# Value matmuls of sixteen attention units in four quarters of the array, with a new instruction order

## The chip, the cores and the metric

The kernel runs on one core of a Trainium2 chip. The metric is the device time of one execution in microseconds; lower is better. Engines are called by their rows in the profile: PE is TensorE (PEld its weight loads), DVE is VectorE, ACT is ScalarE, POOL is GpSimd, and SP is the queue that issues the transfers.

## What is computed

Attention over 4 batches of 8 heads, 768 positions and 64 elements a head, followed by a gated convolution. Each query sees its neighbours within 16 positions and one summary of each of the 24 blocks of 32 positions; the result, with the heads side by side (512 wide), goes through a gate and two 512x512 products.

```python
k_sum = k.reshape(B, H, nb, block, D).max(axis=3)
v_sum = v.reshape(B, H, nb, block, D).mean(axis=3)
scores_l = scale * np.matmul(q, k.transpose(0, 1, 3, 2))
mask_l = np.abs(pos[:, None] - pos[None, :]) < window
scores_s = scale * np.einsum('bhsd,bhnd->bhsn', q, k_sum) + np.log(block)
a = softmax(np.concatenate([np.where(mask_l, scores_l, -1e9), scores_s], axis=-1))
x = np.matmul(a, np.concatenate([v, v_sum], axis=2))
...
for k in range(K):
    gate_pre += conv_w[k][None, None, :] * xp[:, k:k + S, :]
gate = 1.0 / (1.0 + np.exp(-gate_pre))
val = x @ w_val
return gate * val @ w_out
```

## The kernel before, in words

The work is cut into 24 units, numbered 0 to 23 in the code: 4 batches x 3 thirds of a sequence (256 queries) x 2 halves of the heads (two head pairs, r = 0 and 1). Two units make a group g, 0 to 11, in which all 512 columns of 256 positions are there. The order of everything is written out by hand: the string `ORDER` is a list of words, each one call of a small function with its numbers, and each engine runs its share of the calls in that order. Waits between engines come from the data alone.

A unit u goes through these words. `s` (L519) multiplies queries by 120 keys, 16 matmuls in the four quarters of the array (two row halves for the heads, two column halves for the queries). `n` (L536) adds the mask on DVE, eight steps with the row maximum; `e` (L555) takes the exponentials on ACT; `r` (L562) the row sums and reciprocals on DVE; `m` (L567) scales on POOL. `t` (L576) transposes on PE into one PSUM bank, once for each r, and `c` (L581) copies it out on ACT. `x` (L588) multiplies by the values: 16 matmuls of 120 rows into 64 columns each, in the two column halves of the array, into one bank of its own:

```python
dst = xp(u)[h * D : (h + 1) * D, r, i * QT : (i + 1) * QT]
src = pts(u)[:, TPU * r + 2 * (i // 2) + h, (i % 2) * QT : (i % 2 + 1) * QT]
nc.tensor.matmul(dst, v[:KW, i, c0 : c0 + D], src, start=True, stop=g > 0)
```

PE takes an fp32 matmul in two passes, so the trace has 32 records for these 16 calls, and two for each other fp32 one that is no transpose. `Y` (L609) copies x to SBUF on ACT, `X` (L605) writes its rounded head there too, and `Z` (L613) the rest on POOL. `I` (L622) starts the gate with the newest tap on ACT, `T` (L629) adds four more taps on DVE, four dependent instructions for each r, and `G` (L638) takes the tanh on ACT.

A group then goes through `v` (L642, x times w_val, four calls of 12 matmuls), `gf` (L655, gate times val on DVE), `gh` and `gl` (L663, L666, its head on ACT and rest on POOL), `o` (L674, times w_out, two calls), `ob` and `O` (scale on ACT, store). Group 0 computes in plain fp32 with the joined weights `wf` (four calls of `val`, and eight of `out`, each of 128 columns); the other groups use the split weights. The weights come as 64-bit numbers that ACT and DVE turn to fp32: `rb` on ACT, `sh` (L363) and `or` (L367, the join) on DVE, four blocks for each matrix. `ks` (L221) takes the block maxima of the keys on DVE, `kc` (L233) writes them between the keys on POOL, `vp` (L271) sums the blocks of the first batch's values on DVE, `tv` (L244) those of the others on POOL.

Of the eight PSUM banks, scores have two, transposes one, x one, the gate one, and val, out and some small products share three.

Of the kernel before, what the change touches and what calls it, by code (L numbers as in the profile page):

```python
# [22 lines left out]
QT = 64  # L23
# [13 lines left out]
KALLOC = OFF_A + 2 * STEP * (NT // 2 + 1)  # L37
# [7 lines left out]
LATE_INIT = (2, 3, 4, 5)  # L45
# [4 lines left out]
DVE_COPY = ()  # L50
POOL_V = ()
POOL_LOW = ()
# [3 lines left out]
Lk0.0 wz Lk0.1 Mu ez cv W0 Lp0 W1 Lc W2 W3 W4 Lk0.2 W5 Lp1 W6 W7 W8 Mm Lp2 ks0.0 Lk0.3 ks0.1 Lp3  # L56
W9 W10 shc kc0.0 W11 W12 s0.0 W13 n0.0 kc0.1 W14 Ln1 s0.1 ks0.2 W15 e0.0 n0.1 Ln0 kc0.2 ks0.3
W16 s1.0 e0.1 kc0.3 Mi W17 n1.0 r0 vp1.1 W18 W19 s1.1 m0.0 e1.0 n1.1 Lq1 vp0.0 vp1.0 rbc e1.1
t0.0 s2.0 vc1.1 c0.0 s2.1 Lwv1 Ln3 m0.1 vp0.1 vc1.0 vc0.0 vc0.1 W20 W21 t0.1 vb0 hal0 W22 n2.0
shwv1 Lv0 n2.1 Ln2 rbwv1 orc c0.1 vbc0 orwv1 Lq2 Lwv2 W23 s3.0 s3.1 x0.0 e2.0 x0.1 r1 n3.0 vp3.0  # L60
n3.1 vp3.1 e2.1 wcwv1 I0 m1.0 m1.1 t1.0 Y0 vp2.0 vp2.1 r2 Lwv0 c1.0 e3.0 t1.1 Lwv3 Lv1 s4.0 T0.0
vc3.0 vc2.1 vc3.1 vc2.0 s4.1 vb1 n4.0 rbwv2 c1.1 vbc1 n4.1 x1.0 rbwv0 e3.1 rbwv3 wlwv1 m2.1 m2.0
shwv0 shwv2 s5.0 t2.0 x1.1 orwv0 shwv3 orwv2 orwv3 s5.1 Lk1.0 Lk1.1 n5.0 r3 c2.0 Y1 T0.1 n5.1
e4.0 wcwv3 e4.1 v0.1.0 t2.1 v0.0.0 G0 m3.1 wcwv2 Lk1.2 c2.1 wlwv3 m3.0 I1 r4 Lu1.2 v0.1.1 m4.0
F1 Lq3 t3.0 e5.0 m4.1 c3.0 v0.0.1 t3.1 x2.0 e5.1 ks1.1 x2.1 ks1.0 T1.0 c3.1 Lk1.3 wlwv2 X2 Y2
kc1.1 kc1.0 T1.1 ks1.2 t4.1 Lv2 Lu1.1 Lwo1 ks1.3 s6.0 Lq4 s6.1 hal1 tv1.2 x3.0 Lwo0 x3.1 G1 I2
c4.1 Z2 n6.1 n6.0 t4.0 gf0.1 r5 kc1.2 kc1.3 T2.0 X3 Y3 wcwv0 e6.0 s7.0 s7.1 n7.0 gf0.0 T2.1 Z3
# [46 lines left out]
def tile_attention_then_gated_conv(  # L114
# [69 lines left out]
    def ident_make():  # L184
# [619 lines left out]
```

## Time and profile before

| | us |
|---|---|
| median of 3 runs | 238.43 |
| the runs | 238.08 to 238.94 |
| profiled execution, span from its first to its last instruction | 236.1 |
| PE busy | 224.9 (95%) |
| ACT busy | 190.6 (81%) |
| DVE busy | 184.2 (78%) |
| POOL busy | 152.2 (64%) |

The profiled execution is one more execution than the three that were timed; the page gives its own time as the span, which holds nothing of what lies ahead of the first instruction and behind the last.
Busy time is that in which an engine works on an instruction. PE's matmuls are pipelined and overlap, so its busy time is a union of records. A view of waits tells for each engine which other engine's instruction ended its idle time; the chain of waits is followed back from the last instruction.

### The profile page before, as it was taken

To read this page: it belongs to the slowest core of one execution; us is meant where nothing else is said; L and a number is where in the kernel's file an instruction comes from. 1 tells how busy PE (TensorE), PEld (TensorE's weight loads), DVE (VectorE), ACT (ScalarE), POOL (GpSimd) and SP (SyncE) were. 2 spreads that over 40 slices of the span, in tenths; PEclk is the share of its full clock that TensorE was granted. 3 is DMA by queue.
4 is the path that set the end of the run, shared out by engine and by line. 5 is a ranking of instruction groups with operands and counts; after the bars stand their busy time and mean duration, and the time that the engine had idled before them with its cause. 6 is when DMAs were issued, how large, how long until landed. Compare 5 with 4: busy or idle time off the path is not lost.

```text
span 236.1 us, 7464 instructions
## 1 busy us (share of the span) xinstructions
PE 224.9 (95%) x2734; PEld 196.1 (83%) x2736; DVE 184.2 (78%) x698; ACT 190.6 (81%) x620; POOL 152.2 (64%) x222
## 2 busy tenths in 40 slices
PE   7777999998999999999999999999999999999994
PEld 2356787897999889998899799898889898898983
DVE  6899889999989999988899979839568765544710
ACT  2699899998899998999999989598979399347221
POOL 4246369998989896876658859963850845608030
PEclk9999999999999999999999999999999999999999
DMA  6999989939846789392757168711634420202212
GB/s 202 402 408 393 412 280 384 336 115 321 286 170 208 296 254 282 124 310 89 240 98 270 46 186 322 250 40 27 230 77 117 142 95 3 89 3 95 83 56 78
DMA packets 19812, 46.14 MB, mean 195 GB/s; under 512 B 2336, under 2 KB 7200, under 8 KB 19776
## 3 DMA queue, kind: packets, MB, share of 16 engines
q1 hardware_dynamic: 19776, 45.68, 56.6%
q8 instruction: 21, 0.34, 0.6%
q14 instruction: 15, 0.12, 0.1%
HBM read 37.21 MB, written 6.29 MB: 184 GB/s over the span
## 4 chain that ended last, share of the span: by engine, by line
PE 78%; DVE 14%; ACT 2%; DMA 2%; issue 1%; SPq 1%; POOL 0%; DVEq 0%; ACTq 0%; POOLq 0%
PE out L690 28%; PE val L653 24%; PE x L596 9%; PE pt L579 8%; PE s L528 8%; DVE g L633 4%; DVE sn L544 3%; DMA q<-in_qT_dram 2%; DVE ks L225 2%; DVE wf L367 2%; DVE wf L363 1%; PE x L598 1%; DVE gf L659 1%; ACT p L557 1%; SPq L204 1%
## 5 line engine op out<-in xcount | busy, mean ns | idle before, releaser
L633 DVE SCALAR_TENSOR_TENSOR g<-xf,cwt,g 128x256 f32<-128x256 f32 x192 | 93.7, 488 | 24.0 <-ACT g L627 12.7
L557 ACT ACTIVATE p<-sn,nm 128x120 f32<-128x120 f32 x192 | 73.3, 388 | 5.8 <-DVE nm L544 5.8
L569 POOL TENSOR_TENSOR p<-p,ri 128x480 f32<-128x480 f32 x48 | 47.3, 998 | 31.2 <-DVE ri L565 19.9
L653 PE MATMUL val<-xh,wv 128*128 128x256 f32 x352 | 50.8, 287 | 0.0
L653 PEld LDWEIGHTS val<-xh,wv 128*128 128x128 f32 x352 | 44.1, 189 | 0.3 <-issue 0.2
L690 PE MATMUL out<-wo,gh 128*128 128x512 f32 (+1 forms) x184 | 44.0, 381 | 0.0
L544 DVE CUSTOM_DVE_ANT_0 sn<-s,mask 128x120 f32<-128x120 f32 x192 | 41.5, 277 | 3.0 <-PE s L528 2.7
L667 POOL TENSOR_TENSOR gl<-gf,gh 128x512 fp32r<-128x512 f32 x22 | 28.1, 1287 | 21.8 <-ACT gh L664 21.7
L690 PEld LDWEIGHTS out<-wo,gh 128*128 128x128 f32 x184 | 32.8, 188 | 5.9
L586 ACT COPY pts<-pt 120x512 f32<-120x512 f32 x48 | 28.0, 584 | 11.6 <-PE pt L579 11.5
L557 ACT ACTIVATION_READ_ACCUMULATOR p<-sn,nm 128x1 f32 x192 | 37.1, 193 | 0.0
L579 PE MATMUL pt<-ident,p 128*120 128x128 f32 x192 | 30.0, 279 | 2.9 <-ACT pts L586 2.1
L615 POOL TENSOR_TENSOR xl<-xf,xh 128x512 fp32r<-128x512 f32 x22 | 28.4, 1296 | 3.9 <-ACT xf L611 3.2
L596 PE MATMUL x<-pts,v 120*64 120x64 f32 x768 | 30.2, 225 | 0.0
L596 PEld LDWEIGHTS x<-pts,v 120*64 120x64 f32 x768 | 26.2, 137 | 3.9 <-issue 1.5
L528 PE MATMUL s<-k,q 64*64 64x120 f32 x768 | 25.9, 269 | 2.1 <-POOL k L239 0.6
L579 PEld LDWEIGHTS pt<-ident,p 128*120 128x120 f32 x192 | 21.2, 137 | 7.8 <-POOL vpad L287 1.7
L253 POOL TENSOR_TENSOR vT<-vT 128x384 f32<-128x384 f32 (+3 forms) x44 | 25.9, 589 | 2.6
L653 PE MATMUL val<-xl,wv 128*128 128x256 f32 x176 | 27.5, 278 | 0.0
L528 PEld LDWEIGHTS s<-k,q 64*64 64x64 f32 x768 | 19.9, 132 | 7.2 <-issue 2.4
L659 DVE SCALAR_TENSOR_TENSOR gf<-gt,val 128x512 f32<-128x512 f32 x24 | 16.3, 679 | 10.5 <-PE val L653 10.1
L690 PE MATMUL out<-wo,gl 128*128 128x512 f32 (+1 forms) x92 | 23.8, 380 | 0.0
(64 smaller groups left out, 282.9 us busy)
## 6 DMA issues: line engine op xcount, KB each, us to landing
v<-in_vw_dram SPq DMA_DIRECT2D x24, 512.0 KB
k<-in_kT_dram SPq DMA_DIRECT2D x16, 478.0 KB
vT<-in_vT_dram SPq DMA_DIRECT2D x16, 384.0 KB
out_dram<-ob SPq DMA_DIRECT2D x23, 256.0 KB
q<-in_qT_dram SPq DMA_DIRECT2D x11, 512.0 KB
raw_wv<-in_wv_dram SPq DMA_DIRECT2D x4, 512.0 KB
raw_wo<-in_wo_dram SPq DMA_DIRECT2D x4, 512.0 KB
v<-vs SPq DMA_DIRECT2D x36, 48.0 KB
```

The lines of the kernel that those rows point to most:

```text
L528: nc.tensor.matmul(sp(u)[64 * e : 64 * e + 64, h, c * KW : c * KW + KW], qt(g)[64 * h : 64 * h + 64, pr, i * QT : i * QT + QT], ktile[b, p ...
L544: nc.vector.tensor_tensor_reduce(sn(u)[:, n, :], sp(u)[:, h, c * KW : c * KW + KW], mask[:, mv, :], -1.0 / math.sqrt(D), 3.0e38, ALU.add, ...
L557: nc.scalar.activation(pr_(u)[:, n, :], sn(u)[:, n, :], AF.Exp, bias=nm(u)[:, n : n + 1], scale=-1.0, accum_out=rs(u)[:, n, 0:1],)
L569: nc.gpsimd.tensor_tensor(pr_(u)[:, w], pr_(u)[:, w], st["ri", u][:, w].unsqueeze(2).broadcast_to([P, TPU, KW]), ALU.mult,)
L579: nc.tensor.transpose(pt[:KW, i, :], pr_(u)[:, TPU * r + i, :], ident)
L586: nc.scalar.copy(dst, src)
L596: nc.tensor.matmul(dst, v[:KW, i, c0 : c0 + D], src, start=True, stop=g > 0)
L615: nc.gpsimd.tensor_tensor(xl(g)[:, two(hp), :], xf(g)[:, two(hp), HALO:], xh(g)[:, two(hp), :].bitcast(F32), ALU.subtract,)
L633: nc.vector.scalar_tensor_tensor(gp(u)[:, r], xf(g)[:, pr, o : o + SG], cwt[:, pr, o : o + 1], gp(u)[:, r], ALU.mult, ALU.add,)
L653: nc.tensor.matmul(pp[:, r], w, x, start=(n == 0), stop=(n == len(terms) - 1))
L667: nc.gpsimd.tensor_tensor(gl(g)[:, two(cp), :], grp["gf", g, cp], gh(g)[:, two(cp), :].bitcast(F32), ALU.subtract)
L690: nc.tensor.matmul(pp, x, w, start=(n == 0), stop=(n == len(terms) - 1))
```

## The change

- `x` of units 4 to 19 (the fifth to the twentieth) is cut in two along its 120 rows: 64 and 56. Each of its matmuls becomes two, in two row halves of the array, so that the four quarters are used; the row halves write to two PSUM banks (`xp(u, 0)` and `xp(u, 1)`). `Y` copies the first to SBUF, and a new word `Ya` adds the second to it on DVE. `X` and `I` of these units read SBUF.
- The bank of x is given up: transposes and x take turns in two banks (`ps_t`, 2 buffers).
- Queries of group 0 stand behind the keys of batch 0 in one array (`kq`), so that four loads bring both. The weights are loaded by rows rather than by columns.
- `v` of group 0 is cut by the two units, `o` of group 0 by rows (one matmul of 512 columns for each call, added up over four calls).
- `n`, `e`, `T`, `I` and `r` are cut to smaller words, so that others can stand between their pieces. Some work changes its engine: 12 `X`, 12 `gh` and four weight casts go from ACT to POOL (`Xp`, `ghp`, `wcp`); 14 half `I`, five `Y`, two `X`, four `c` and five `ob` from ACT to DVE (`Id`, `Yd`, `Xd`, `cd`, `obd`); half of the value sums of batch 0 from DVE to POOL (`vt`). The scaled bits of w_val lie in PSUM.
- `ORDER` is another one.

The core of the diff (of `ORDER` and of what only renames or splits a function, a line or two):

```diff
-LATE_INIT = (2, 3, 4, 5)
+QUARTERS = tuple(range(4, 20))
+LATE_INIT = (2, 3, 4, 5) + QUARTERS
...
-W16 s1.0 e0.1 kc0.3 Mi W17 n1.0 r0 vp1.1 W18 W19 s1.1 m0.0 e1.0 n1.1 Lq1 vp0.0 vp1.0 rbc e1.1
+kc0.1 s0.1 W11 n0.1.1 n0.1.0 ks0.2 n0.0.0 n0.0.1 Lk0.3 Ln1 Lq1 Ln0 Ln3 Lc Lwv2 Ln2 Lwv0 ks0.3
...
-    ps_t = ctx.enter_context(tc.tile_pool(name="ps_t", bufs=1, space=bass.MemoryType.PSUM))
-    ps_x = ctx.enter_context(tc.tile_pool(name="ps_x", bufs=1, space=bass.MemoryType.PSUM))
+    ps_t = ctx.enter_context(tc.tile_pool(name="ps_t", bufs=2, space=bass.MemoryType.PSUM))
...
+        if b == 0:
+            nc.sync.dma_start(t, kq[pr])
+        else:
+            nc.sync.dma_start(t[:, :KTOT], kT[b - 1, pr])
...
+        if nm[:2] == "wv":
+            home, tag, bufs = ps_p, "pp", 3
...
-        nc.sync.dma_start(
-            raw.rearrange("p (k c) -> p k c", c=n), wcols[nm][:, :, k * n : k * n + n]
-        )
+        nc.sync.dma_start(raw, wrows[nm][k])
...
-    def xp(u):
-        return bank(ps_x, "x", u, [P, 2, SG])
+    def xp(u, half=0):
+        key = "x", u, half
+        if key not in st:
+            st[key] = ps_t.tile([P, 2, SG], F32, tag="pt", name=f"x_{u}_{half}")
+        return st[key]
...
+    def mm_x_quarters(u, r):
+        b, th, hp, g = of(u)
+        for i in range(TPU):
+            for half, rows in enumerate((slice(0, 64), slice(64, KW))):
+                for h in range(2):
+                    c0 = (2 * hp + r) * P + h * D
+                    nc.tensor.matmul(
+                        xp(u, half)[h * D : (h + 1) * D, r, i * QT : (i + 1) * QT],
+                        vtile[g][rows, i, c0 : c0 + D],
+                        pts(u)[rows, TPU * r + 2 * (i // 2) + h, (i % 2) * QT : (i % 2 + 1) * QT],
+                        start=True,
+                        stop=True,
+                    )
...
+    def x_head(u, eng=None):
+        b, th, hp, g = of(u)
+        src = xf(g)[:, two(hp), HALO:] if u in QUARTERS else xp(u)
+        (eng or nc.scalar.copy)(xh(g)[:, two(hp), :], src)
...
+    def x_add(u):
+        b, th, hp, g = of(u)
+        dst = xf(g)[:, two(hp), HALO:]
+        nc.vector.tensor_tensor(dst, dst, xp(u, 1), ALU.add)
...
+    def tap(u, r, o):
+        b, th, hp, g = of(u)
+        pr = 2 * hp + r
+        nc.vector.scalar_tensor_tensor(
+            gp(u)[:, r], xf(g)[:, pr, o : o + SG], cwt[:, pr, o : o + 1], gp(u)[:, r],
+            ALU.mult, ALU.add,
+        )
...
-            terms = [(grp["gf", g, ci // 2][:, ci % 2, rows], wblock(cb)[:, ci]) for ci in range(4)]
+            terms = [(grp["gf", g, cb // 2][:, cb % 2, rows], wf[:, cb])]
+            start, stop = cb == 0, cb == 3
...
-        "x": mm_x, "X": x_head, "Y": x_full, "Z": x_rest, "I": ginit, "T": taps, "G": gate,
+        "x": mm_x, "Ya": x_add, "X": x_head, "Y": x_full, "Z": x_rest, "I": ginit, "T": tap, "G": gate,
...
+        "cd": on(pcopy, dcopy), "Xd": on(x_head, dcopy), "Xp": on(x_head, pcast), "Yd": on(x_full, dcopy),
+        "ghp": on(g_head, pcast), "Id": on(ginit, scaled_dve), "obd": on(out_scale, scaled_dve),
```

What the new order does to two engines, at the places of which the prediction speaks. A name's number is that of a buffer's use; `x8` counts calls.

DVE ahead of the fourth join of the output weights (`wf<-sc_wo`, `wf`), before:

```order
L363 TENSOR_SCALAR wf<-raw_wo_771 128x512
L367 SCALAR_TENSOR_TENSOR wf<-sc_wo_952,wf 128x512
L363 TENSOR_SCALAR wf<-raw_wo_732 128x512
L367 SCALAR_TENSOR_TENSOR wf<-sc_wo_878,wf 128x512
L363 TENSOR_SCALAR wf<-raw_wo_924 128x512
L367 SCALAR_TENSOR_TENSOR wf<-sc_wo_981,wf 128x512
L659 SCALAR_TENSOR_TENSOR gf_0_1004<-gt_977,val_0_904 128x512
L564 TENSOR_REDUCE ri_1006<-rs_114 128x8
L565 RECIPROCAL ri_1006<-ri_1006 128x8
L249 TENSOR_REDUCE vsT_3_1027<-vT_3_1016 128x24
L363 TENSOR_SCALAR wf<-raw_wo_998 128x512
L367 SCALAR_TENSOR_TENSOR wf<-sc_wo_1009,wf 128x512
```

and with the change:

```order
L677 SCALAR_TENSOR_TENSOR g_823<-xf_787,cwt,g_823 128x256
L396 SCALAR_TENSOR_TENSOR wf<-sc_wo_877,wf 128x512
L392 TENSOR_SCALAR wf<-raw_wo_757 128x512
L596 RECIPROCAL ri_884<-ri_884 128x8
L657 TENSOR_TENSOR xf_889<-xf_889,x_1_971 128x2x256
L396 SCALAR_TENSOR_TENSOR wf<-sc_wo_1013,wf 128x512
L392 TENSOR_SCALAR wf<-raw_wo_759 128x512
L573 ISA sn_1037,nm_1038<-s_959,mask 128x120
L573 ISA nm_1038 128x1
L573 ISA sn_1037,nm_1038<-s_959,mask 128x120
L573 ISA nm_1038 128x1
L396 SCALAR_TENSOR_TENSOR wf<-sc_wo_1029,wf 128x512
```

The block sums `vsT` went behind the join and the gated product as well; the first sum of x (`xf<-xf,x_1`) and two score steps (`sn`) came ahead of it, and taps (`g<-xf,cwt,g`) stand singly between other work.

PE at unit 9, from its x to the next two transposes, before:

```order
L596 MATMUL x_1705<-pts_1609,v_1408 64x64 x16
L528 MATMUL s_1747<-k_2_1247,q_1496 64x120 x8
L528 MATMUL s_1747<-k_3_1516,q_1496 64x120 x8
L579 MATMUL pt_0_1764<-ident,p_1451 120x128 x4
L653 MATMUL val_0_1692<-xh_1258,wv 128x256 x8
L653 MATMUL val_0_1692<-xl_1550,wv 128x256 x4
L653 MATMUL val_0_1802<-xh_1641,wv 128x256 x8
L653 MATMUL val_0_1802<-xl_1774,wv 128x256 x4
L579 MATMUL pt_0_1815<-ident,p_1569 120x128 x4
```

and with the change (the last four of the 16 rows of x, two calls each):

```order
L621 MATMUL x_0_1728<-pts_1677,v_1189 64x64 x2
L621 MATMUL x_1_1731<-pts_1677,v_1189 64x64 x2
L621 MATMUL x_0_1728<-pts_1677,v_1189 64x64 x2
L621 MATMUL x_1_1731<-pts_1677,v_1189 64x64 x2
L705 MATMUL val_1_1684<-xh_1502,wv 128x256 x8
L705 MATMUL val_1_1684<-xl_1527,wv 128x256 x4
L610 MATMUL pt_0_1822<-ident,p_1397 120x128 x4
L705 MATMUL val_0_1827<-xh_1502,wv 128x256 x8
L705 MATMUL val_0_1827<-xl_1527,wv 128x256 x4
L705 MATMUL val_0_1827<-xh_1502,wv 128x256 x8
L705 MATMUL val_0_1827<-xl_1527,wv 128x256 x4
L610 MATMUL pt_1_1875<-ident,p_1397 120x128 x4
```

The scores of unit 13 (`s`) stood behind x and stand ahead of it now; the x of one unit writes to two tiles, `x_0` and `x_1`, and the two transposes that follow, `pt_0` and `pt_1`, come into the same two banks, the first behind one call of val and the second behind three.

## Rows read from the trace of the kernel before

**Rows 1.** The page's head.

```profile
span 236.1 us, 7464 instructions
```

**Rows 2.** Windows: us, busy time (count) of PE, PEld, DVE, ACT, POOL, PEclk, DMA share, GB/s.

```profile
58.90:140.00 81.10, 81.06 (x1039) 73.22 (x1040) 75.24 (x303) 75.96 (x254) 64.20 (x94) 1.00 0.62 204
140.00:232.90 92.90, 92.84 (x964) 83.35 (x962) 56.01 (x184) 64.45 (x189) 49.91 (x53) 1.00 0.33 108
```

**Rows 3.** Waits of DVE (us, times, longest), 4.3 to 58.9 us and 58.9 to 102.

```profile
DVE sn L544 <- PE s L528: 2.0, 3, 1.1
...
DVE g L633 <- ACT g L627: 0.4, 1, 0.4
```

**Rows 4.** Chain that ended last: start us, us, what.

```profile
55.55 0.20 DVE ri L565
...
57.30 1.59 DVE wf L367
58.94 4.73 PE out L690 x40
...
107.42 2.73 PE out L690 x12
...
232.93 0.38 ACT ob L700
```

**Rows 5.** Timeline of PE from 117.7 us: start us, us, instructions.

```profile
117.73 1.05 PE L528 MATMUL s<-k,q 64*64 64x120 f32 x32
118.71 1.15 PE L596 MATMUL x<-pts,v 120*64 120x64 f32 x32
119.79 0.65 PE L579 MATMUL pt<-ident,p 128*120 128x128 f32 x4
120.20 1.17 PE L653 MATMUL val<-xh,wv 128*128 128x256 f32 x8
...
121.66 0.60 PE L579 MATMUL pt<-ident,p 128*120 128x128 f32 x4
122.02 1.17 PE L653 MATMUL val<-xh,wv 128*128 128x256 f32 x8
```

**Rows 6.** The page's costliest groups: busy us, mean ns of one.

```profile
L596 PE MATMUL x<-pts,v 120*64 120x64 f32 x768 | 30.2, 225 | 0.0
L528 PE MATMUL s<-k,q 64*64 64x120 f32 x768 | 25.9, 269 | 2.1 <-POOL k L239 0.6
```

**Rows 7.** Groups by line and form, DVE's reductions.

```profile
L225 DVE TENSOR_REDUCE ks<-k 128x24 f32<-128x768 f32 x16 | 14.7, 937 | 0.1
L274 DVE TENSOR_REDUCE vpad<-vT 128x12 f32<-128x384 f32 x8 | 4.0, 540 | 0.0
L249 DVE TENSOR_REDUCE vsT<-vT 128x24 f32<-128x768 f32 x1 | 0.9, 903 | 0.0
```

**Rows 8.** Timeline of DVE from 96.9 us.

```profile
96.92 0.68 DVE L659 SCALAR_TENSOR_TENSOR gf<-gt,val 128x512 f32<-128x512 f32 x1
97.51 2.06 DVE L633 SCALAR_TENSOR_TENSOR g<-xf,cwt,g 128x256 f32<-128x256 f32 x4
99.48 0.28 DVE L544 CUSTOM_DVE_ANT_0 sn<-s,mask 128x120 f32<-128x120 f32 x1
...
99.68 0.28 DVE L544 CUSTOM_DVE_ANT_0 sn<-s,mask 128x120 f32<-128x120 f32 x1
```

**Rows 9.** Groups by line and form, ACT's copy of x.

```profile
L611 ACT COPY xf<-x 128x512 f32<-128x512 f32 x24 | 14.1, 586 | 0.7 <-PE x L598 0.7
```

**Rows 10.** Groups by line and form, POOL.

```profile
L615 POOL TENSOR_TENSOR xl<-xf,xh 128x512 fp32r<-128x512 f32 x22 | 28.4, 1296 | 3.9 <-ACT xf L611 3.2 <-ACT xh L607 0.7
...
L239 POOL COPY k<-ks 128x84 f32<-128x84 f32 x16 | 4.1, 254 | 12.0 <-DVE ks L225 12.0
...
L287 POOL COPY vpad<-vpad 128x12 f32<-128x12 f32 x8 | 1.4, 193 | 1.9 <-DVE vpad L274 1.8
```

**Rows 11.** Window of 0.04 us, the score matmuls (L528) alone.

```profile
117.72:117.76 0.04, 0.03 (x4) 0.03 (x4) 1.00 0.80 307
```

More of the change, by code (lines that the diff above doesn't have):

```diff
@@ L392, in w_low @@
         if wide:
[L393 removed]
+            low_bits(nc.vector, wf[:, k], wraw[nm, k])
     def w_join(nm, k):
@@ L521, in mm_s @@
         pr = 2 * hp + r
+        qs = qt(g)[:, pr] if g else ktile[0, pr][:, KTOT:]
         for j in range(TPU // 2):
@@ L646, in val_mm @@
         pp = pss["val", g, cp]
+        cis = range(4) if hp is None else (2 * hp, 2 * hp + 1)
         if g in FP32_G:
-            terms = [(wblock(2 * cp + r)[:, ci], xf(g)[:, ci, HALO:]) for ci in range(4)]
+            terms = [(wf[:, ci, cols], xf(g)[:, ci, HALO:]) for ci in cis]
         else:
-            terms = [(w[:, ci], xh(g)[:, ci, :]) for ci in range(4) for w in (wh, wl)]
-            terms += [(wh[:, ci], xl(g)[:, ci, :]) for ci in range(4)]
+            terms = [(w[:, ci, cols], xh(g)[:, ci, :]) for ci in cis for w in (wh, wl)]
+            terms += [(wh[:, ci, cols], xl(g)[:, ci, :]) for ci in cis]
+        seen = open_.setdefault((g, cp), [])
+        seen.append((r, hp))
+        first, last = hp is None or len(seen) == 1, hp is None or len(seen) == 4
         for n, (w, x) in enumerate(terms):
-            nc.tensor.matmul(pp[:, r], w, x, start=(n == 0), stop=(n == len(terms) - 1))
+            nc.tensor.matmul(
+                pp[:, r], w, x, start=first and n == 0, stop=last and n == len(terms) - 1
+            )
     def gated(g, cp):
@@ L661, in gated, with g_head @@
         )
-    def g_head(g, cp):
-        nc.scalar.copy(gh(g)[:, two(cp), :], grp["gf", g, cp])
+    def g_head(g, cp, eng=None):
+        (eng or nc.scalar.copy)(gh(g)[:, two(cp), :], grp["gf", g, cp])
     def g_rest(g, cp):
@@ L689, in out_mm @@
         for n, (x, w) in enumerate(terms):
-            nc.tensor.matmul(pp, x, w, start=(n == 0), stop=(n == len(terms) - 1))
+            nc.tensor.matmul(
+                pp, x, w, start=start and n == 0, stop=stop and n == len(terms) - 1
+            )
     obs = {}
     def out_scale(g, si, *part):
+        put = scaled_act
+        if part and callable(part[-1]):
+            part, put = part[:-1], part[-1]
         ob = obs[(g, si) + part] = wk.tile(
@@ L728, in tile_attention_then_gated_conv @@
             ops[pre + n] = fn
+    for pre, f, eng in (
+        ("wcp", w_head, pcast),
+    ):
+        for n, fn in both(f, eng).items():
+            ops[pre + n] = fn
     for word in ORDER.split():
```

324 lines of the change are left out of this document (170 added, 154 removed).

## The prediction

> **What bounds the kernel now.** The page's head gives a span of 236.1 us [rows 1] and an engine table that puts TensorE far ahead, but a busy share does not say who waits for whom. The windows tell more: from 58.9 to 140 us TensorE is busy for 81.06 of 81.10 us and VectorE for 75.24; after 140 TensorE stays full (92.84 of 92.90) while VectorE falls to 56 [rows 2]. What is missing of VectorE's first stretch is mostly the few tens of ns between its instructions, because its waits add up to only 2.0 us from 4.3 to 58.9, and 0.4 us from 58.9 to 102 [rows 3]. So two engines are full at once until about 140 us. The chain of waits names the handover: up to 58.94 it goes through VectorE, last the join of the fourth block of the output weights (L367), then through TensorE to the last output, whose final scaling starts at 232.93 [rows 4]. TensorE is thus unbroken for 174.0 us, and starts that stretch when VectorE is done with the group-0 weights. The change has to be priced at both places.
>
> The profiled execution spans 236.1 us; the median of the three runs is 238.43, 2.3 us more, which I take as work around the span that the change leaves alone.
>
> **The x matmuls themselves: nothing.** A unit's x runs in two column halves of the array, 32 records of 64 columns, so 16 x 64 = 1024 columns through each half, and takes 1.08 us from its start to the next start [rows 5]. In quarters it is 64 records in four streams: again 16 x 64 = 1024 columns through each. The scores s already run in quarters: 32 records of 120 columns, 960 per stream, in 0.98 us [rows 5]. By that price 1024 columns take 1.05 us, as now. The same columns at the same rate exclude a real gain. From above, if only two quarters could run at once, a unit would take 2.16 us, which is +1.08 x 16 = 17 us; I take the nearest row, s, which has the same four quarters, the same two banks by row half and the same 64-column weights.
>
> **Fewer changes of the array's split: -2.2 us.** The s records are 0.27 us each [rows 6] and the group of 32 ends after 1.05, so its last one starts 0.78 after its first; x starts 0.20 after that, where s's own eight groups of four step by 0.11. An x record is 0.23 us [rows 6], the last of 32 starts 0.92 after the first, and the transposes start 0.16 later, where x steps by 0.06. Transposes to val, whole array to whole array, lose nothing: 0.36 us for four of them [rows 5]. So one change costs 0.09 us, and the four transposes behind x take 0.41 instead of 0.36: another 0.05 for a slow first step. I use 0.13 (bounds 0.09 and 0.15). Counted in the two orders (quarters, column halves, whole array), TensorE changes its split 85 times before and 61 times now; behind the last group-0 steps it is 52 and 35. 17 x 0.13 = 2.2 us.
>
> **VectorE up to the weights' join: -3.0 us.** By the order, these instructions no longer stand ahead of the fourth join: four of the eight v sums (0.54 each), one v sum of 128x768 (0.90) [rows 7] and one gated product (0.59 from its start to the next [rows 8]): 3.65. New ahead of it: two copies of transposes and the first x sum (two operands, 128x512, one from PSUM, like the gated product: 0.6 each) and two score steps (0.20 each [rows 8]): 2.2. The taps: four take 1.97 us from the first start to the next instruction's (97.51 to 99.48), the last row is 0.49 long and the four end after 2.06, so taps behind taps step by 0.52 and a tap before something else by 0.40 [rows 8]. The order ahead of the join has 19 such tap-behind-tap pairs before and 6 now: 13 x 0.13 = 1.7. Reductions overlap their successors by some 0.08, which takes 0.15 off. Sum -3.0, so the join ends near 55.9.
>
> Behind the join TensorE now has unit 5's x and one group of v transposes more (1.08 + 0.4 = +1.5), because they came ahead of it before. The last five group-0 output calls, 4.73 us for 40 records [rows 4], become five of one 512-column matmul each: the same columns, estimate no change within 0.4. So its unbroken stretch is 174.0 + 1.5 - 2.2 = 173.3, and it would end at 55.9 + 173.3 = 229.2 instead of 232.9: -3.7.
>
> **What the second bank costs: +0.9 us.** x and the transposes now share two banks. The first transposes behind x wait for ACT's copy of the first bank (0.59 [rows 9]), the second ones for VectorE's add. The place where VectorE is latest by the order is unit 9. From the join to that add it has 40 taps (19 x 0.52 + 21 x 0.40 = 18.3), 44 score steps x 0.20 = 8.9, five row sums with their reciprocals (the reciprocal 0.20 [rows 4], the sum of the same size ahead of it about as long, less their overlap: 0.32) = 1.6, five adds, four gated products, a copy and a scaling = 11 x 0.6 = 6.6, five key maxima (0.94 each [rows 7], less overlap) = 4.5, one v sum 0.8: 40.7, and 0.4 of waits as in the same stretch before. 55.9 + 41.1 = 97.0. TensorE from the last group-0 steps to those transposes has 4.7 for group 0, four out halves x 2.73 [rows 4] = 10.9, eight val x 1.40 (120.20 to 121.66 with the step out [rows 5]) = 11.2, eight transposes x 0.38 = 3.0, five blocks of s and x x (0.98 + 1.08 - 0.13) = 9.7, v transposes 0.4: 39.9, which is 96.0 with the join's semaphore. It waits about 0.9 us there. Bounds: none, if VectorE's adds cost no more than the 0.5 of a tap; 3 us, if VectorE idles 2 us more than before. A later unit that comes late waits in the same time, not in addition, and after 140 us VectorE has idle time to spare.
>
> **Work moved off ACT.** ACT hands 12 x casts, 12 gate casts and four weight casts to POOL, and 14 half gate starts and some copies to VectorE; ACT's own time is no bound. POOL's copies take 193 ns for 12 elements and 254 for 84: 0.85 ns an element, 0.62 us for 512. From above stands its two-input subtraction of 512, 1.30 [rows 10]. I take 0.65: 28 casts are 18 us on an engine that was idle for 84. VectorE in all gets 16 adds, 30 moved pieces, less four v sums and 68 tap pairs (160 to 92): about +14 us, covered by its idle time behind 140 us, except as priced.
>
> **The start.** Keys and queries of group 0 come as four loads instead of eight (and the weights in whole rows); the second one ends later for the first scores and earlier for the others. VectorE waits 2.0 us in that stretch [rows 3]; I take the same, within 1 us either way.
>
> Sum: -3.7 + 0.9 = -2.8 on the span, so **235.6 us** on the median's scale.
>
> **The rivals.**
> A, slower: the banks. Each unit's x needs both banks free, and the next transposes need both back, ACT's copy first and then VectorE's add, 0.59 + 0.6 and two semaphores, about 1.3 us. Where val or out does not cover it, TensorE stands. The forecast has this once; if it holds in every quartered unit for 0.5 us, it is +8 in place of 0.9: 242.7. From 0.23 us a unit on (3.7 / 16) the gain is gone. For it: VectorE, which frees the second bank, is full until 140. Against: the order puts one or more val or out calls (1.4 to 2.7 us) between x and the second transposes.
> B, slower: quarters that don't overlap. At two at a time 252. In the window of 0.04 us around the start of one s, four of its matmuls start [rows 11]; that speaks against any queue for quarters. The Trainium skill ("TensorE: Matmul & The Clock Gate", section "Wait — 56ns, not 53.3ns?") states that starts never come closer than about 25 ns, however few the columns. By that rule alone, an estimate, 64 records take 1.6 us, +0.55 a unit, and the end comes near 244. The trace disagrees for different quarters, with those four starts in 0.04 us. From +0.23 us a unit on, B eats the gain too.
> C, no change: POOL's casts cost 1.30 each. Between the eleventh and the fourteenth unit POOL then has six of them among some 30 us of other work, and TensorE waits some 2 us longer: near 237.6.
> D, more gain: the packed loads and val of group 0 in halves fill the start, where TensorE still waits on and off; another 2.5 us off gives 233.
>
> **How the numbers follow.** Forecast 0.60 (own range 233.5 to 238), A 0.11, B 0.06, C 0.10, D 0.13. A measurement of this kernel tells 0.3% (0.7 us) from no change, so faster is below 237.7 and slower above 239.1. Faster: 0.55 of the forecast and D = 0.68. Same: 0.05 of the forecast and 0.08 of C = 0.13. Slower: A, B and 0.02 of C = 0.19. The range 232.0 to 240.5 leaves out B, half of A and the tail of D.
>
> **What would show it.** Right: a unit's x and s together in about 1.9 us, x records in quarters at 1.05 a unit; the fourth join near 56; VectorE's waits small until 100; a wait of TensorE for the add of 1 us or less in all; casts on POOL of 0.6 to 0.7 us; TensorE's last output near 230. Wrong: x at 1.6 or more a unit (B), many waits of transposes for the add or for ACT's copy (A), a join later than 58, or POOL's casts above 0.95 with waits of the transposes for POOL (C).

## The result, and the profile after

The changed kernel takes 236.32 us (median of 20 executions, 235.25 to 238.92), the kernel before 238.38 beside it. The ratio of the undisturbed executions is 0.990 (95% interval 0.988 to 0.993). 235.6 was forecast, with a range of 232.0 to 240.5: the direction, the size and the two places hold. One thing that no row of before shows was missed: in half of the executions the mean granted clock of TensorE is below 0.995, and in the profiled one it is the start in which it falls.

The profiled execution took 237.33 us and is one of that half. Its page gives the span and, in the row of 40 slices, the granted clock of TensorE in tenths:

```profile
span 235.2 us, 8434 instructions
...
PEclk9979999999999999999999999999999999999999
```

The third slice is at 0.7. In windows (the last three numbers of each row are PEclk, DMA share and GB/s) the stretch from 13 to 16 us has 0.50, the lower of the two levels, 1.2 instead of 2.4 GHz; the two windows behind it answer to [rows 2]:

```profile
8.00:13.00 5.00, 2.52 (x31) 1.04 (x23) 4.53 (x29) 3.78 (x19) 1.50 (x6) 0.99 1.02 408
13.00:16.00 3.00, 2.86 (x29) 1.96 (x33) 2.69 (x14) 2.59 (x14) 2.92 (x5) 0.50 1.04 419
...
57.30:140.00 82.70, 82.70 (x1375) 72.60 (x1376) 78.42 (x308) 69.17 (x241) 73.02 (x107) 1.00 0.64 207
140.00:232.10 92.10, 91.61 (x1113) 82.18 (x1112) 72.73 (x221) 50.07 (x160) 55.52 (x64) 1.00 0.35 110
```

TensorE is again unbroken from the handover on (82.70 of 82.70, then 91.61 of 92.10), and VectorE is fuller than before: 72.7 of the last 92.1 us, where it had 56 of 92.9. What TensorE did ahead of the fall is in its timeline: it stood 1.49 us ahead of the third scores and 1.13 ahead of the fourth.

```profile
11.05 0.64 PE L558 MATMUL s<-k 64*64 64x120 f32 x16 [1.49 <-DVE nm L573]
11.62 0.39 PE L335 MATMUL warm_out<-warm 128*128 128x512 bf16 x1
13.14 1.08 PE L558 MATMUL s<-k 64*64 64x120 f32 x16 [1.13 <-POOL k L272]
```

The chain of waits has the handover and the last scaling, as [rows 4] has them for before:

```profile
56.22 1.00 DVE wf L396
57.22 0.04 issue
57.26 3.70 PE out L745 x8
...
232.13 0.38 ACT ob L219
```

The fourth join ends at 57.22 (58.89 before) and TensorE's stretch is 174.9 us long (174.0 before).

The same kernel was run once more for the study. An execution of it with the clock at 1.00 throughout, 235.53 us and a span of 233.4, has these rows of the chain:

```profile
55.04 1.00 DVE wf L396
56.04 0.04 issue
56.09 3.70 PE out L745 x8
...
230.34 0.38 ACT ob L219
```

Join at 56.04, stretch 174.25. Against the span of before that is -2.7, against the profiled execution with the fall -1.8 (1.2 at the join, 0.6 in the stretch). The time from outside the span is not the same in the two kernels: an execution of before takes 1.7 us more than its span (75 executions, 1.66 to 1.88), one of the changed kernel 2.1 to 2.2. So of the 2.7 us of span some 2.3 are left in the time at full clock.

The waits of TensorE in the profiled execution hold none for VectorE's add or for ACT's copy; behind the join there is one for the summary rows of unit 16's values, which come late behind a load: 0.4 us by this view, 0.6 from one record of x to the next.

```profile
PE s L558 <- POOL k L272: 1.7, 3, 1.1
...
PE s L558 <- DVE nm L573: 1.5, 1, 1.5
...
PE x L621 <- DMA v<-vs: 0.4, 1, 0.4
```

The timeline of TensorE around the x of unit 7 shows x and s side by side, 0.98 and 0.93 us from start to start, together 1.91; before they took 0.98 and 1.08 [rows 5]:

```profile
76.01 1.16 PE L621 MATMUL x<-pts,v 64*64 64x64 f32 x64
76.99 1.00 PE L558 MATMUL s<-k,q 64*64 64x120 f32 x32
77.92 1.45 PE L745 MATMUL out<-wo,gh 128*128 128x512 f32 x5
```

And the groups by form give POOL's casts and VectorE's add, to be set beside the bounds of [rows 10] and the gated product of [rows 8]:

```profile
L648 POOL CAST xh<-xf 128x512 fp32r<-128x512 f32 x12 | 7.8, 654 | 0.0
L718 POOL CAST gh<-gf 128x512 fp32r<-128x512 f32 x12 | 7.3, 614 | 7.1 <-DVE gf L713 7.1
...
L657 DVE TENSOR_TENSOR xf<-xf,x 128x512 f32<-128x512 f32 x16 | 10.8, 676 | 0.1
```

From the trace the time to spare at each bank is read as the start of the transposes less the end of the add or copy that freed it. The least behind an add is 0.21 us at unit 9, then 0.42 at unit 4, 0.50 at 11 and 14, 0.54 at 12, 0.63 at 5, 0.76 at 15; TensorE waits at none.

### The profile page after: what moved, and what is told of

It reads as the page before. It is cut to its first block, busy times and chain, and to the rows that moved or that the text cites. A ratio compares the mean times of both kernels' runs of the same rounds, so it can differ in the third digit from the quotient of the medians.

```text
span 235.2 us, 8434 instructions
## 1 busy us (share of the span) xinstructions
PE 224.5 (95%) x3200; PEld 191.8 (82%) x3200; DVE 202.3 (86%) x740; ACT 165.3 (70%) x562; POOL 173.5 (74%) x262
## 4 chain that ended last, share of the span: by engine, by line
PE 64%; DVE 18%; DMA 7%; ACT 5%; issue 2%; SPq 2%; POOL 1%; DVEq 0%; ACTq 0%; POOLq 0%
PE out L745 22%; PE val L705 20%; PE s L558 7%; PE pt L610 6%; PE x L621 6%; DVE g L677 5%; DMA v<-in_vw_dram 4%; DVE sn L573 4%; DVE wf L396 3%; ACT p L586 3%; DMA k<-in_kq_dram 2%; PE x L639 2%; DVE ks L258 1%; DVE wf L392 1%; DMA v<-vs 1%
## 5 line engine op out<-in xcount | busy, mean ns | idle before, releaser
L573 DVE CUSTOM_DVE_ANT_0 sn<-s,mask 128x120 f32<-128x120 f32 x192 | 44.0, 275 | 3.6 <-PE s L558 3.0
L745 PE MATMUL out<-wo,gh 128*128 128x512 f32 (+1 forms) x184 | 45.4, 389 | 0.0
L613 ACT COPY pts<-pt 120x512 f32<-120x512 f32 x44 | 24.8, 583 | 15.7 <-PE pt L610 15.7
L610 PE MATMUL pt<-ident,p 128*120 128x128 f32 x192 | 26.8, 276 | 0.1
L610 PEld LDWEIGHTS pt<-ident,p 128*120 128x120 f32 x192 | 22.3, 138 | 4.2 <-issue 1.7
L558 PE MATMUL s<-k,q 64*64 64x120 f32 x704 | 24.5, 270 | 0.6 <-DVE ri L596 0.6
L684 ACT ACTIVATE gt<-g 128x512 f32<-128x512 f32 x24 | 14.3, 596 | 14.8 <-DVE g L677 14.8
L705 PEld LDWEIGHTS val<-xl,wv 128*128 128x128 f32 x176 | 23.6, 189 | 0.0
L558 PEld LDWEIGHTS s<-k,q 64*64 64x64 f32 x704 | 18.5, 135 | 4.8 <-issue 3.0
L745 PEld LDWEIGHTS out<-wo,gl 128*128 128x128 f32 x92 | 16.9, 188 | 3.4
```

Of the source, the lines that this page charges most:

```text
L558: nc.tensor.matmul(sp(u)[64 * e : 64 * e + 64, h, c * KW : c * KW + KW], qs[64 * h : 64 * h + 64, i * QT : i * QT + QT], ktile[b, pr][64 * ...
L573: nc.vector.tensor_tensor_reduce(sn(u)[:, n, :], sp(u)[:, h, c * KW : c * KW + KW], mask[:, mv, :], -1.0 / math.sqrt(D), 3.0e38, ALU.add, ...
L610: nc.tensor.transpose(pt[:KW, i, :], pr_(u)[:, TPU * r + i, :], ident)
L613: (eng or nc.scalar.copy)(pts(u)[:, TPU * r : TPU * r + TPU], st.pop(("pt", u, r))[:KW])
L705: nc.tensor.matmul(pp[:, r], w, x, start=first and n == 0, stop=last and n == len(terms) - 1)
L745: nc.tensor.matmul(pp, x, w, start=start and n == 0, stop=stop and n == len(terms) - 1)
```

## The experiments

The theory: the time is the end of the fourth join plus TensorE's unbroken stretch; the first fell because VectorE has less ahead of it, the second hardly moved, because fewer changes of the array's split pay for the work that came behind the join. The rivals: the banks, the casts, the taps at no price, and the clock. Medians are of the executions named; "at full clock" means a granted clock of 0.997 or more over the execution. The experiments were timed in three series, each with the kernel before beside it: 238.01, 237.97 and 237.90, so times of different series can be set side by side.

**x in halves again**

```diff
     def mm_x(u, r):
-        if u in QUARTERS:
-            return mm_x_quarters(u, r)
...
-Ya4 Ya5 Ya6 Ya7 Ya8 Ya9 Ya10 Ya11 Ya12 Ya13 Ya14 Ya15 Ya16 Ya17 Ya18 Ya19
```

> The changed kernel with x of all units in two column halves and one bank again; the adds on VectorE are gone, the order is the same otherwise. Theory (the gain of the quarters is in the fewer changes of the array's split): by the order TensorE changes its split 87 times instead of 61, behind the group-0 steps 58 instead of 35; 23 x 0.13 = +3.0 us, less up to 0.6 because one add ahead of the join of the weights is gone: 2.4 to 3.0 us slower than the changed kernel, about 239. Rival (the second bank and its 16 adds of 0.6 us cost more than the changes of split): faster than the changed kernel, 235 or less. Rival (quarters neither gain nor cost): the same within 0.7 us.

Measured: 238.33 us (12 executions), ratio to before 1.001 (0.998 to 1.003); at full clock 237.46 against 235.65 for the changed kernel, +1.8. The handover and the end in its profiled execution, which has the fall of the clock too:

```profile
55.72 0.62 DVE wf L391
56.34 0.04 issue
56.39 1.98 PE out L738 x4
```

The join ends 0.88 earlier than in the profiled execution of the changed kernel (56.34 against 57.22; the add ahead of it is gone, and its own piece of the chain is 0.62 long instead of 1.00), and the last scaling starts at 234.03, so the stretch is 177.6, 2.8 longer, or 3.4 if the wait of 0.6 us at unit 16 is left out of the other. 23 changes of split at 0.13 were to be 3.0.

The traces show where it goes. With halves x starts 0.19 us behind the last s and s 0.15 behind the last x, with quarters 0.08 and 0.04. Blocks in which the x of one unit and the s of another alternate tell a price per change from a price per unit. Here is one of them, first with halves, then with quarters (the execution at full clock); between the two rows shown x and s alternate, with three changes from one to the other:

```profile
68.69 0.69 PE L632 MATMUL x<-pts,v 120*64 120x64 f32 x16
...
71.06 1.18 PE L698 MATMUL val<-xh,wv 128*128 128x256 f32 x8
```

```profile
68.16 0.69 PE L621 MATMUL x<-pts,v 64*64 64x64 f32 x32
...
70.08 1.20 PE L705 MATMUL val<-xh,wv 128*128 128x256 f32 x8
```

That is 2.37 us from start to start against 1.92. A block with one change from x to s (or back) takes 2.06 against 1.91, one with two 2.22 against 1.92, and the x of unit 17, which stands between whole-array work, 1.08 against 1.09. So every change costs 0.15 us, x itself costs the same in either form, and 23 changes are 3.45 us, which is what TensorE has more. Of that the join gives back 0.9. With x in halves the rest of the change, in this order, is worth nothing in the median, and 0.5 us at full clock (237.46 against 237.98 for before in the same series).

**All taps in fours**

```diff
-T4.1.0 T4.1.1 n9.0.1 T4.1.2 T4.0.0 T4.0.1 T4.0.2 T4.0.3 rr8 T4.1.3
+n9.0.1 T4.0.0 T4.0.1 T4.0.2 T4.0.3 rr8 T4.1.0 T4.1.1 T4.1.2 T4.1.3
```

(VectorE's words at one of some 40 such places)

> The changed kernel with the four taps of each row pair together again, at the place of the last of them. Theory (a tap behind a tap of the same accumulator costs 0.13 us of VectorE, and VectorE sets the join of the weights): 14 more such pairs ahead of the fourth join, 14 x 0.13 = 1.8, so the join goes from 57.2 to about 59; from there to the add of unit 9, which had 0.2 us to spare, 19 more pairs (2.5 us), up to the add of unit 15 28 more beyond the first 28; in all 4 to 6.5 us slower, 240 to 243. Rival (the pairs are hidden ahead of the join, only the later ones count): join unmoved, 1 to 3 us slower. Rival (the pitch does not matter because VectorE waits elsewhere): no change.

Measured: 256.89 us (5 executions, with clocks of 0.973 to 0.986), +20.6, a miss by far. The join ends at 60.83, 3.6 later, where 1.8 was expected, and then both engines wait for each other:

```profile
DVE sn L569 <- PE s L554: 8.7, 8, 3.5
DVE ri L589 <- ACT p L582: 5.6, 8, 1.5
DVE xf L653 <- ACT xf L648: 4.3, 4, 2.0
```

The edit did two things at once: it paired the taps, and it moved score steps and adds ahead of taps, to times at which their inputs were not there yet. It says how tight the order is and nothing clean of the pairs. The next run keeps the places of the gates.

**Taps in fours ahead of the join only** (on the kernel with more warm-up matmuls, below)

```diff
-rr4 T1.0.0 rv4 T1.0.1 ks1.3 T1.1.1 n6.1.0 n6.0.1 T1.0.2 n6.0.0 ks1.2 T1.0.3 n6.1.1 T1.1.2 gf0.0 T1.1.3
+rr4 rv4 ks1.3 T1.1.0 T1.0.0 T1.0.1 T1.1.1 n6.1.0 n6.0.1 n6.0.0 ks1.2 n6.1.1 T1.0.2 T1.0.3 T1.1.2 T1.1.3 gf0.0
...
-T2.0.0 T2.1.0 rv5 T2.0.1 shwo0 T2.1.1 gf0.1 T2.1.2 T2.0.2 orwo0 T2.1.3 shwo1 rr6 T2.0.3 orwo1
+rv5 shwo0 T2.0.0 T2.1.0 T2.0.1 T2.1.1 gf0.1 rr6 T2.1.2 T2.0.2 T2.1.3 T2.0.3 orwo0 shwo1 orwo1
```

> The kernel with ten more warm-up matmuls, and in it the taps of units 1 and 2 in two fours each rather than between other work; all stay ahead of the fourth join, nothing crosses it. Ten more taps stand behind a tap. Theory (0.13 us for each such pair, and VectorE alone sets the join): the join ends at 56.0 + 1.3 = 57.3 and the time goes up by 0.9 to 1.3 us, to 236.6 to 237.0. Rival (the pairs are covered, VectorE waits for other engines there): join and time unmoved within 0.3. The run with all taps in fours was 20 us slower, which the pitch alone does not give; this one keeps the place of the gates.

Measured: join at 57.45, +1.42; time 237.75 (12 executions), the profiled one 1.4 us of span above the kernel that it was made from, the median about 2.0. That the join moved by what ten pairs were to cost is in part a coincidence. Summed from each start to the next start, the 24 taps ahead of the join take 11.5 us here and 10.3 there, so the pairs give 1.2. But the row sums went ahead of the taps too, and VectorE waits for ACT there: 0.32 us at 35 us and, first row, 0.99 at 49, where the other kernel has one wait of 0.78 (second row); and the first shift of the output weights takes 0.35 us instead of 1.00. These two nearly cancel.

```profile
49.31 0.17 DVE L589 TENSOR_REDUCE ri<-rs 128x8 f32<-128x16 f32 x1 [0.99 <-ACT p L582]
```

```profile
43.11 0.28 DVE L569 CUSTOM_DVE_ANT_0 sn<-s,mask 128x120 f32<-128x120 f32 x1 [0.78 <-ACT p L582]
```

The term itself is read better from the two kernels of the prediction: the taps ahead of the join take 11.96 us before and 10.26 with the change, 1.70 less. The profiled execution has a fall of the clock as well, and not in the start but at 52 to 56 us (0.57 to 0.58), while TensorE works on group 0; it then starts the last group-0 calls at 57.95, 0.5 behind the join. The ninth slice of the row has it:

```profile
PEclk9999999997999999999999999999999999999999
```

Why the median, 237.94 for the nine executions at full clock, moved by 0.6 to 0.8 more than the join is open.

**More warm-up matmuls**

```diff
-W12 W13 W14 W15 W16 s1.0
+W12 W13 W14 W15 W16 W24 W25 W26 W27 W28 W29 s1.0
...
-s1.1
+W30 W31 W32 W33 s1.1
```

> The changed kernel with ten more warm-up matmuls, six ahead of the third scores and four ahead of the fourth, where TensorE stood still for 1.49 and 1.13 us and the granted clock fell to 0.50 from 13 to 16 us in the profiled execution. Theory (the fall of the clock delays the first scores, and with them VectorE and the join, by about 1.2 us in those executions that have it): the clock is 1.00 in all executions, the join comes near 56, the median falls by 0.8 to 1.2 us to about 235.3. Rival (VectorE and the loads set the join whatever the clock): the same time within 0.3 us, with a clock of 1.00.

Measured: 235.69 (5 executions), the clock at 1.00 in each. The same two stretches, and the join:

```profile
8.00:13.00 5.00, 4.74 (x44) 1.98 (x37) 4.42 (x27) 3.66 (x19) 1.38 (x6) 1.00 1.03 408
13.00:16.00 3.00, 2.45 (x53) 1.80 (x55) 3.00 (x15) 3.00 (x17) 2.92 (x5) 1.00 1.04 422
```

```profile
55.04 1.00 DVE wf L392
56.04 0.04 issue
56.08 3.70 PE out L741 x8
```

Join at 56.04 instead of 57.22, as in an execution of the changed kernel without the fall.

**The changed kernel and the one with more warm-up once more, side by side**

> The changed kernel once more, unchanged, beside the next three on the same chip. Of 20 executions 10 had a granted clock under 0.995 and took 236.8 us in the median, the other 10 took 235.65. Theory (the fall of the clock early on is the whole difference): again both kinds, about 1.1 us apart, median between 235.6 and 236.8. Rival (the first measurement's spread came from something else): the clock does not sort the times.

> The kernel with ten more warm-up matmuls once more. Theory: every execution at a clock of 1.00, median 235.5 to 235.8, that is 0.5 to 1 us below the changed kernel in this call. Rival (the first five executions were luck): the clock falls in some executions and the median is that of the changed kernel.

Measured: 235.76 and 235.94 (6 executions each): no difference. The changed kernel had a lower clock (0.993) in one of six here, with the longest of its times, 237.07. In both series together it had 11 of 26 executions under 0.995, the kernel with more warm-up none of 11 (0.998 or more). The traces say where: of five traces of kernels without the ten matmuls four have a clock of 0.50 to 0.59 from 13 to 16 us, of eight with them none. So the fall in the start costs some 1.2 us where it comes, and the ten matmuls keep it away there. They don't keep the clock up elsewhere: of the six kernels made from this one, four had executions under 0.995 (14 of 42 in these four). Two traces show such an execution, and in both the clock falls later, behind pauses of TensorE that the edit made longer (1.8 us at 50 us with the taps in fours, where the kernel that it was made from has 0.6). How often it falls differs between series, and as a faster kernel the variant is shown in the first series alone. The rest of the spread at full clock, 0.8 to 1.5 us, has at least one other source: the profiled execution of the second variant waits 0.6 us for the summary rows at unit 16, that of the changed kernel beside it not at all.

**The load of group 8's values earlier**

```diff
-F7 ob4.0 O4.0 Lu3.2 Lq10 Lu3.0 x14.1 x14.0 Lv8
+F7 Lv8 ob4.0 O4.0 Lu3.2 Lq10 Lu3.0 x14.1 x14.0
```

> The changed kernel with the load of the values of group 8 three loads and one store earlier on the queue. There TensorE stood 0.6 us within x of unit 16, behind the fill of the summary rows, which waited for this load. Theory (TensorE's stretch is unbroken otherwise, so what the wait costs comes back): 0.4 to 0.6 us faster. Rival (the transposes of unit 17, which had 0.25 us to spare there, wait instead): 0 to 0.3 us faster.

Measured: 236.58 (12 executions, six of them with the fall of the clock), 235.42 at full clock against 235.65. In its profile the wait is gone; 0.2 us is below what these runs can tell. Since the wait is not in every execution, it could not give 0.6.

**The adds two instructions later** (on the kernel with more warm-up matmuls)

```diff
-Ya14 T12.1.3 n18.0.1
+T12.1.3 n18.0.1 Ya14
```

(13 units by two instructions, and unit 11 by one)

> The kernel with ten more warm-up matmuls, and the add of 13 of the 16 units two VectorE instructions later (one for unit 11; units 9 and 16 stay), that is 0.4 to 1.0 us later. The transposes that need the bank had 0.42 us to spare at unit 4, 0.50 at 11 and 14, 0.55 at 12, 0.64 at 5, 0.77 at 15, over 1.1 elsewhere. Theory (waits for the bank do not add up: who waits once is late enough for the next): 0.2 to 0.6 us slower. Rival A of the prediction (each unit pays its own): some six units by 0.2 to 0.4, 1.5 to 2.5 us slower. Rival (the bank is not what the transposes need): no change.

Measured: 238.85 (12 executions), +2.9 to +3.2 on 235.94 and 235.69: neither the 0.2 to 0.6 of the theory nor quite rival A's 1.5 to 2.5. The waits of TensorE:

```profile
PE pt L606 <- DVE xf L653: 3.2, 5, 1.4
```

By the records TensorE stands ahead of transposes behind the adds of units 4, 5, 12, 15 and 17, 0.4 to 1.4 us each, and the waits add up. The 1.4 of unit 4 lie ahead of the last group-0 calls, which start 0.6 later; behind them there are 1.8 us in four waits, all transposes together take 1.0 longer, and 0.7 go to waits for others: about the 4.0 by which the profiled span is longer. Why a unit that is held up doesn't gain room for the next is not tested. What fits is that VectorE falls back too: its score steps wait 4.2 us for TensorE's scores in eight waits, where 2.3 in four stood before, so the next late add is late again. A transpose that waited starts 0.05 to 0.15 us behind the add's end; of the 0.2 to spare at unit 9 only the rest is room.

**VectorE 1.2 us longer behind the join**

```diff
-T3.1.0 n8.0.0
+T3.1.0 n8.0.0 n8.0.0 n8.0.0 n8.0.0
```

> The kernel with ten more warm-up matmuls, with one pair of score steps of unit 8 done four times, so VectorE has 6 x 0.2 = 1.2 us more just behind the fourth join and none ahead of it. Theory (VectorE is full from there to the add of unit 9, which had 0.2 us to spare): the join stays at 56.0, TensorE waits about 1.0 us by 98 us, time +0.8 to +1.2. Theory with credit (VectorE waits for other engines on the way and makes it up): 0 to +0.3. Rival of the waits adding up (each later unit pays as well): more than +1.5.

Measured: 236.88 (12 executions), +0.9 to +1.2 on 235.94 and 235.69; the join stays (55.91).

```profile
PE s L555 <- DVE nm L570: 0.9, 2, 0.7
```

The size is the theory's, the place another: TensorE waits 0.7 us at 62 us (the other 0.2 of this row lie in the start), in front of the scores of unit 9, whose bank these very steps have to read first. At the transposes of unit 9 the 0.2 us to spare are unchanged.

**The join later**

```diff
-shwo3 n8.1.1 orwo3
+shwo3 shwo3 shwo3 n8.1.1 orwo3
```

> The kernel with ten more warm-up matmuls, with the shift of the fourth block of the output weights done three times instead of once (the result is the same each time), so VectorE has about 1.2 us more ahead of the fourth join (0.6 each). Theory (the join starts TensorE's unbroken stretch and both engines run on from there): join at 57.2, time +1.1 to +1.3, about 236.9. Rival (TensorE has slack later, or VectorE has idle time ahead of the join): 0 to +0.5.

Measured: the two shifts put the join off by 2.0 instead of 1.2 (one of them has 1.37 us of the chain), it ends at 58.02, and the time at full clock is 237.64, +1.7 to +2.0. Five of 12 executions had a lower clock and 239.3. What is put ahead of the join comes out at the end nearly in full.

**The join two score steps earlier, and the load earlier** (on the kernel with more warm-up matmuls)

```diff
-shwo3 n8.1.1 orwo3
+shwo3 orwo3 n8.1.1
```

(and `Lv8` as in the run of the load alone)

> The kernel with ten more warm-up matmuls, the load of the values of group 8 three loads and a store earlier, and the fourth join of the output weights ahead of the two score steps that stood before it (0.4 us). Theory (VectorE's join starts TensorE's unbroken stretch): join at 55.6, the time 0.3 to 0.6 us below the 235.7 of the kernel with warm-up matmuls alone. Rival (the add of unit 9, with 0.2 us to spare, takes the gain): 0 to 0.2 us.

Measured: 236.28 (12 executions, spread to 241), no gain. The join started 0.35 earlier and ended 0.13 earlier. The timelines of VectorE and POOL show why; first this kernel, then the one that it was made from:

```profile
54.61 1.29 DVE L392 SCALAR_TENSOR_TENSOR wf<-sc_wo,wf 128x512 uint32<-128x512 uint32 x1
54.19 1.16 POOL L596 TENSOR_TENSOR p<-p,ri 128x480 f32<-128x480 f32 x1
```

```profile
54.96 1.07 DVE L392 SCALAR_TENSOR_TENSOR wf<-sc_wo,wf 128x512 uint32<-128x512 uint32 x1
54.32 1.16 POOL L596 TENSOR_TENSOR p<-p,ri 128x480 f32<-128x480 f32 x1
```

POOL's multiplication ends at 55.35 and 55.48, and the join 0.55 behind it in both (55.90 and 56.03): with both operands in SBUF it gets on only when POOL is done. So its end was set by POOL, and two score steps ahead of it were free. The joins of w_val, whose scaled bits lie in PSUM since the change, don't show this: in the execution of the changed kernel at full clock one of them took 0.69 us from 24.09 on, in the middle of POOL's multiplication (23.67 to 24.84).

**The casts back on ACT** (on the kernel with more warm-up matmuls)

```diff
-Xp4 Xp5 Xp7 Xp8 ghp3.0 ghp4.0
+X4 X5 X7 X8 gh3.0 gh4.0
```

(six of the 24 words: 12 casts of x and 12 of the gated product, at their places in the order)

> The kernel with ten more warm-up matmuls, and the 12 casts of x and the 12 of the gated product back on ACT. They took 0.65 and 0.61 us on POOL, 15 us in all; ACT gets about 14.5. Theory (neither engine sets the end, but ACT's copies free the banks that the transposes need, and some had only 0.5 to 0.8 us to spare): 0 to 1 us slower. Rival (POOL's 15 us were a hidden price of the change): faster by 0.5 or more. Rival (ACT becomes a bound): slower by 2 or more.

Measured: 251.8 (6 executions), 249.8 at full clock, +14. ACT is busy 70% of the span in the changed kernel, yet the casts of the gated product and x now stand in its queue among copies and exponentials. In the profiled execution (254.3 us, at a clock of 0.971) POOL waits 22.4 us for ACT's cast of x, where the kernel that it was made from has 1.2, and TensorE for what is behind that on POOL:

```profile
PE pt L606 <- POOL p L596: 5.0, 3, 3.0
PE val L701 <- ACT xh L644: 3.0, 2, 2.3
PE pt L606 <- POOL xf L487: 1.7, 1, 1.7
```

The order was made for POOL, and the words were left in their places; an order made for ACT may do better, and was not tried.

## Why the prediction was right, and where it was not

**The x matmuls: right.** x and s together take 1.91 us, as said, and x alone 0.93 to 1.09 from start to start. Where no change of split is saved, at unit 17, it takes 1.09 in quarters and 1.08 in halves.

**Fewer changes of split: right, a little low.** 0.13 a change was taken, with bounds of 0.09 and 0.15; the two kernels with x in halves and in quarters give 0.15. Against before, s and x of the stretch take 1.3 us less at full clock with one unit of x (1.08) more in it, so -2.4 for a forecast of -2.2.

**The join: right, term by term.** -3.0 to 55.9 was forecast; 56.04 at full clock, -2.85. VectorE's rows ahead of the join, from start to start, give -1.70 for the taps (forecast -1.7), -3.4 for the sums and the gated product that went behind it (-3.65), and +1.9 for the copies, the add and the score steps that came ahead (+2.2). What was in no term comes to +0.3 net. The shifts and joins of the weights, which POOL makes long or short, take 10.4 us in both kernels; that their changes cancel was not foreseen.

**The second bank: wrong.** A wait of 0.9 us at unit 9 was in the sum; there is none, and 0.2 to spare. VectorE's side was right: 41.1 us from the join to the end of unit 9's add were worked out, 40.95 measured (57.22 to 98.17). TensorE's was low: 40.1 against 41.1 (57.26 to 98.38). The wrong step is the prices of TensorE's own work. From start to start in that stretch the four out halves take 11.6 us (10.9 taken), the eight val 11.7 (11.2), the transposes 3.2 (3.0) and the v transposes 0.5 (0.4), while group 0 takes 4.5 (4.7) and s and x 9.6 (9.7). Before, an out half that stood alone took 2.74; in the new order they take 2.74 to 2.94, and why is open. The error cancelled, because what TensorE doesn't wait it works: the stretch is 174.25 at full clock, 174.2 with the wait in the forecast. That the missing work had just the size of the wait is luck.

**"A later unit that comes late waits in the same time, not in addition": wrong.** It decided nothing, because no unit waits. But it put rival A too low: adds later by 0.4 to 1.0 us cost about 3. The banks don't cost, because the order leaves 0.2 to 0.8 us at each of seven places, and at these places that is all the room there is.

**Casts on POOL: right** (0.65 and 0.61 for an estimate of 0.65); rival C did not come. That ACT's own time is no bound was right in busy time and misleading as a reason: the same 24 casts on ACT cost 14 us at their places in its queue.

**Rival B: not seen.** Four records of x in four quarters start within a window of 0.06 us, and the 64 of unit 7 take 0.98 us. The Trainium skill ("TensorE: Matmul & The Clock Gate", section "Wait — 56ns, not 53.3ns?") has starts never closer than some 25 ns, which would be 1.6 us a unit, an estimate. The trace disagrees for matmuls in different quarters.

**Rival D: not seen.** The join lies where the sum had it.

**The time outside the span: wrong, and lucky.** 2.3 us were taken as work that the change leaves alone. That was the median of three executions less the span of another one; an execution of before has 1.7 us more than its own span, one of the changed kernel 2.1 to 2.2. The mix came out near the changed kernel's value, so 235.6 meets the 235.65 at full clock more closely than its terms deserve. Why the changed kernel has more outside is open (with the casts back on ACT it is 1.7 again).

**The start: wrong by omission.** It was put at no change within 1 us either way. It held for VectorE's work, but not for the clock: TensorE got longer pauses ahead of the third and fourth scores (1.49 and 1.13 us, 0.63 and 0.31 before), and in some executions its clock fell to 0.50 for some 3 us, which delays scores, VectorE and the join by 1.2. The kernel before has 1.00 in those stretches of its trace, and was below 0.995 in 3 of the 75 executions beside the experiments. It is why the median is 236.3 and not 235.65.

## What to carry to other kernels

Where two engines are full at once, find the last handover between them and price a change at that place and in the stretch behind it; what is put ahead of it, or just behind it on the other engine, comes out at the end nearly in full. Read the room at each shared bank from the trace (start of the user less end of the releaser): instructions moved by more than that room made a new wait in each of five units here. To tell a price per change from a price per unit, compare places that have none, one, two and three of the changes. A busy share of 70% on an in-order queue is not yet room, so try a move of work at its real place in the order, and look at the granted clock of the first stages in several executions, not in the profiled one alone.

## What the runs showed of the hardware

- Between s and x in the same quarters nothing is lost: x starts 0.08 us behind the last s and s 0.04 behind the last x, against 0.19 and 0.15 with x in column halves.
- The clock may or may not fall with the same pauses: behind pauses of 1.49 and 1.13 us it was 0.50 from 13 to 16 us in the profiled execution of the changed kernel, and behind the same 1.49 and 1.13 it stayed at 1.00 in the execution at full clock. With ten more matmuls in these pauses it was 1.00 there in all eight traces.
- The join of 128x512 output weights, both operands in SBUF, took 0.69 us where POOL was idle or started behind it. Where it started while POOL worked it took up to 1.58 (the fourth join of before), and where it took more than 0.70 its end was 0.55 behind POOL's. With one operand in PSUM it took 0.67 to 0.69 beside a working POOL. The Trainium skill ("SBUF — State Buffer", section "Terms") says that VectorE and GpSimd share a port pair that one of them holds for a whole instruction, while the other is blocked; these rows agree.
- A change of split between s and x costs 0.15 us, by blocks with one, two and three changes in the kernels with x in halves and in quarters. The Trainium skill ("TensorEngine Tiling (Array Packing)", section "Key Properties") says that changing the tiling mode drains TensorE; these rows agree.
